# Score products of two heads on one array: 64-row matmuls and pairwise loads in a top-k attention kernel

## The chip, the cores and the metric

One core of a Trainium2 chip. The metric is device time in microseconds from the start of the program to its end. Engines are named as in the profile: PE is TensorE (PEld its weight loads), DVE is VectorE, ACT is ScalarE, POOL is GpSimd, SP issues the transfers.

## The reference

Attention in which each query keeps its 32 largest scores, followed by a gated feed-forward part over all rows. The first has batch 8, 8 heads, 576 rows and head size 64; the second 4608 rows, width 512 and inner width 1536.

```python
scores = scale * np.matmul(q, k.transpose(0, 1, 3, 2))
kth = np.partition(scores, -top_k, axis=-1)[..., -top_k:-top_k + 1]
scores = np.where(scores >= kth, scores, -1e9)
attn = softmax(scores)
x = np.matmul(attn, v)            # heads side by side: 4608 x 512
gate = 1.0 / (1.0 + np.exp(-(x @ w_gate)))
out = (gate * (x @ w_val)) @ w_out
```

All inputs and the output are float32.

## The kernel before, in words

**Tiles and steps.** A batch has four pairs of heads. For each pair the 576 rows are cut into four tiles of 128 and one of 64 (`i == NT`), in which both heads' last 64 rows share one tile. One pair and one tile make a step; there are 160, of them 128 with two full tiles (one per head) and 32 with last rows. `groups` gives their order: the first two batches are each cut into two groups (tiles 0 and 1, then 2 to 4), the other six batches are a group each. Within a group all tiles of a pair come before the next pair.

**Precision.** TensorE's fast format (float32r) holds fewer bits than float32, so a float32 operand is held as a high part (a rounded copy, made on ACT) and a low part (the rest, subtracted on POOL). Keys are loaded twice, one copy above the other on the 128 partitions; after the split (lines 147 and 148) the upper 64 partitions hold the high part and the lower 64 the low part. The queries of a step are loaded with the same doubling, 2 x 128 columns, and split into `qh` and `ql` over all partitions (lines 158 and 159). One matmul over 128 rows thus multiplies `qh` with both parts of the keys, a second one `ql`.

**Scores** (line 177). For each head, the 576 keys are cut into halves of 288, and each half takes two matmuls. A head's four matmuls fill the one score buffer in PSUM (`ps_s`, two banks), which ACT reads out with one copy (line 184) before the next head's may begin. The last-rows tile has ten matmuls in one go, as the second head's keys are rolled by 64 columns.

**Selection.** DVE finds the 32nd largest score of each row (lines 237 to 253, with a subtraction on POOL at line 249), ACT takes exponentials, and DVE masks and sums them (line 196). TensorE transposes the weights (line 273), and `weigh` multiplies them with the values (lines 289 to 298): one matmul whose 128 output rows serve both heads, the others with 64 output rows, one head in each half.

**Feed-forward part** (`ffn`, lines 331 to 361). A group's rows are ready when its last step is done. Its work is handed out in pieces between the steps, so that it stays 640 rows behind the attention (`BEHIND`). The weights, given in double precision, are split once near the start of the program and written to memory.

**Order of the work.** `fetch` asks for a pair's keys and values two steps ahead, `ask` for a step's queries four steps ahead, `begin` makes the scores two steps ahead (lines 369 to 400). All these loads are issued on SP, together with those of the feed-forward weights and the stores. From this order and a simulated timing, the compiler of the kernel's language fixes the order of each engine's instructions, which doesn't change at run time. Buffers are counted by the pools of lines 62 to 76.

If a row's count of scores lies outside its bounds, everything is computed a second time in a general way (lines 433 to 445).

Of the kernel before, what the change touches and what calls it, by code (L numbers as in the profile page):

```python
# [10 lines left out]
F32 = mybir.dt.float32  # L11
# [9 lines left out]
# scores are held times SHRINK, far under 1 (a power of two, exact)  # L21
SHRINK = 2.0**-60
# [4 lines left out]
def tile_topk_attention_then_gated_ffn(  # L27
# [10 lines left out]
    B, H, _, S = k.shape  # L38
    D = P // 2
    HALF = S // 2  # L40
    NP = H // 2
# [39 lines left out]
    # place of a row's 32nd largest among the 8 largest under the bound, by its count  # L81
# [58 lines left out]
    def load_keys(b, p, nm):  # L140
        """Both heads' transposed keys, a part over the other on the partitions, and their values."""
        ks = []
        for h in (2 * p, 2 * p + 1):
            raw = bkr.tile([P, S], F32, tag="kraw", name=f"kraw_{nm}_{h}")
            nc.sync.dma_start(raw, k[b, h])
            kt = bk.tile([P, S], F32R, tag="k", name=f"k_{nm}_{h}")
            nc.scalar.activation(kt, raw, AF.Copy)
            nc.gpsimd.tensor_tensor(kt[D:], raw[D:], kt[D:], op=ALU.subtract)
            ks.append(kt)
        vt = bv.tile([P, 11, D], F32, tag="v", name=f"v_{nm}")  # L150
        nc.sync.dma_start(vt, v[b, p].rearrange("p (c d) -> p c d", d=D))
        return ks, vt

    def load_queries(b, i, p):
        raw = bqr.tile([P, 2 * P], F32, tag="qraw", name=f"qraw_{b}_{i}_{p}")
        nc.sync.dma_start(raw, q[b, i, p])
        qh, ql = [bq.tile([P, 2 * P], F32R, tag=t, name=f"{t}_{b}_{i}_{p}") for t in ("qh", "ql")]
        nc.scalar.activation(qh, raw, AF.Copy)
        nc.gpsimd.tensor_tensor(ql, raw, qh, op=ALU.subtract)  # L159
        return qh, ql  # L160

    def scores(qs, ks, i, nm):
        """Scores of one tile of each head (i < NT), or of both heads' last rows in one tile."""
        J = 2 if i < NT else 1
        s = bs.tile([P, 2, S], F32, tag="s", name=f"s_{nm}")
        for j in range(J):
            ps = ps_s.tile([P, 2, 512], F32, tag="s", name=f"pss_{nm}_{j}")
            for half in range(2):
                # a head, the first column, their number, the first key
                parts = [(j, 0, HALF, half * HALF)]  # L170
                if i == NT:
                    # the second head's keys are rolled by REM
                    m = S - REM - HALF
                    parts += [(1, 0, HALF, REM)] if half == 0 else [(1, 0, m, REM + HALF), (1, m, REM, 0)]
# [189 lines left out]
    def run(general):  # L364
# [19 lines left out]
        for m in range(max(FETCH, ASK)):  # L384
            if m < FETCH:
                fetch(m)
# [109 lines left out]
```

## Time and profile before

| | |
|---|---|
| median of 3 runs | 1689.44 us |
| lowest and highest | 1687.72 and 1690.73 us |
| span of the profiled execution | 1685.6 us |
| the profiled execution's own time | listed as its span alone; 3.8 us under the median |
| mean granted TensorE clock | 0.976 of full speed |

The profile is of one execution; all its rows count microseconds from the first instruction. Busy time is a union: matmuls that overlap are counted once, so TensorE's cost of a matmul is read from the distance of its start to the next start. In a row such as `128*64 128x256` the first pair of numbers is the size of the weights (rows of the array by columns of output rows) and the second that of the moving operand.

### The profile page before, as it was taken

How to read it: one execution, taken by the hardware profiler on the slowest of the kernel's cores; microseconds unless marked ns; L12 is line 12 of the kernel's file. 1: busy time of each engine (PE TensorE's matmuls, PEld its weight loads, DVE VectorE, ACT ScalarE, POOL GpSimd, SP SyncE). 2: the span in 40 equal slices, each digit the busy share in tenths (PEclk: the TensorE clock that was granted, in tenths of full speed). 3: DMA queues.
4: the chain of work that ended last, by engine and by line, in shares of the span. 5: the costliest groups of instructions: out<-in, count | busy, mean ns of one | idle time of the engine just before them, and what ended most of it. 6: DMA issues, size and time to landing. Idle time of an engine off the chain costs nothing.

```text
span 1685.6 us, 36209 instructions
## 1 busy us (share of the span) xinstructions
PE 1575.0 (93%) x11506; PEld 1398.7 (83%) x11506; DVE 1521.8 (90%) x6802; ACT 1166.2 (69%) x2467; POOL 1052.7 (62%) x1187
## 2 busy tenths in 40 slices
PE   5665799999999989999999999999999999999998
PEld 2333598888989868998899999999999898999998
DVE  7999999999999999999999999999999999995000
ACT  7787777776777667776676767777776776765222
POOL 6766667767666766576764676576756675564233
PEclk8788899999999989999999999999999999999999
DMA  8777586756776543334433444434534353333543
GB/s 303 257 237 236 206 290 245 271 205 242 251 265 213 210 129 116 138 136 139 163 132 130 136 156 147 134 133 149 170 132 153 124 166 130 118 106 110 195 156 125
DMA packets 86026, 297.37 MB, mean 176 GB/s; under 512 B 9536, under 2 KB 38208, under 8 KB 62784
## 3 DMA queue, kind: packets, MB, share of 16 engines
q1 hardware_dynamic: 85824, 294.95, 51.1%
q8 instruction: 93, 1.52, 0.4%
q14 instruction: 109, 0.89, 0.2%
HBM read 266.60 MB, written 28.31 MB: 175 GB/s over the span
## 4 chain that ended last, share of the span: by engine, by line
PE 49%; DVE 35%; ACT 3%; issue 2%; POOL 1%; POOLq 0%; ACTq 0%; DVEq 0%
PE pz L332 8%; PE pz L331 8%; PE pz L333 8%; DVE e L196 7%; DVE cand L237 7%; DVE tops L252 5%; DVE over L248 5%; PE pss L177 5%; PE pt L273 4%; PE po L351 3%; PE po L353 3%; PE po L352 3%; DVE pick L253 3%; DVE tops L241 3%; PE po L292 3%; DVE cand L243 3%
## 5 line engine op out<-in xcount | busy, mean ns | idle before, releaser
L331 PE MATMUL pz<-xh,w 128*128 128x288 f32 (+2 forms) x1536 | 461.9, 301 | 3.1 <-DVE gf L337 1.5
L332 PE MATMUL pz<-xl,w 128*128 128x288 f32 (+2 forms) x1536 | 459.4, 299 | 0.1
L333 PE MATMUL pz<-xh,w 128*128 128x288 f32 (+2 forms) x1536 | 458.5, 299 | 0.0
L249 POOL TENSOR_TENSOR u<-s,over 128x1152 f32<-128x1152 f32 (+1 forms) x160 | 354.3, 2214 | 74.0 <-DVE over L248 70.2
L237 DVE MAX8 cand<-s 128x8 f32<-128x72 f32 x2304 | 355.3, 216 | 7.0 <-ACT s L184 6.7
L196 DVE SCALAR_TENSOR_TENSOR e<-s,st,e 128x576 f32<-128x576 f32 x288 | 300.8, 1065 | 0.1
L331 PEld LDWEIGHTS pz<-xh,w 128*128 128x128 f32 x1536 | 289.3, 188 | 9.0 <-issue 3.5
L332 PEld LDWEIGHTS pz<-xl,w 128*128 128x128 f32 x1536 | 289.2, 188 | 3.9 <-issue 3.5
L333 PEld LDWEIGHTS pz<-xh,w 128*128 128x128 f32 x1536 | 289.2, 188 | 2.7 <-issue 2.7
L202 ACT ACTIVATE e<-e,st 128x576 f32<-128x576 f32 x288 | 209.4, 771 | 83.1 <-DVE st L200 82.5
L339 POOL TENSOR_TENSOR gl<-gf,gh 128x288 fp32r<-128x288 f32 (+2 forms) x192 | 163.1, 850 | 153.7 <-ACT gh L338 145.8
L192 ACT ACTIVATE e<-s,st 128x576 f32<-128x576 f32 x288 | 210.2, 774 | 35.0 <-POOL st L190 34.1
L351 PE MATMUL po<-gh,w 128*128 128x288 f32 (+2 forms) x768 | 224.4, 302 | 6.3 <-DVE gf L337 3.9
L248 DVE TENSOR_SCALAR_CACHE_REDUCE over<-s,tops 128x576 bf16<-128x576 f32 x288 | 228.5, 798 | 1.1
L352 PE MATMUL po<-gl,w 128*128 128x288 f32 (+2 forms) x768 | 227.6, 299 | 0.6 <-POOL gl L339 0.5
L353 PE MATMUL po<-gh,w 128*128 128x288 f32 (+2 forms) x768 | 226.1, 297 | 0.0
L177 PE MATMUL pss<-k,qh 128*128 128x288 f32 (+2 forms) x672 | 199.7, 314 | 23.5 <-ACT s L184 16.4
L184 ACT ACTIVATE s<-pss 128x576 f32<-128x576 f32 x288 | 185.8, 645 | 47.2 <-PE pss L177 24.2
L252 DVE MAX8 tops<-u 128x8 f32<-128x576 f32 x288 | 204.3, 744 | 2.2 <-POOL u L249 1.4
L274 ACT ACTIVATE et<-pt 128x384 f32<-128x384 f32 x384 | 180.5, 491 | 35.5 <-PE pt L273 33.9
L273 PE MATMUL pt<-ident,e 128*128 128x128 f32 x1152 | 189.7, 281 | 7.7 <-ACT e L202 4.0
L177 PE MATMUL pss<-k,ql 128*128 128x288 f32 (+2 forms) x672 | 190.4, 302 | 0.4 <-POOL ql L159 0.4
(82 smaller groups left out, 3380.3 us busy)
## 6 DMA issues: line engine op xcount, KB each, us to landing
w<-ws SPq DMA_DIRECT2D x180, 1024.0 KB, 5.0
kraw<-in_k_dram SPq DMA_DIRECT2D x80, 288.0 KB, 3.2
qraw<-in_q_dram SPq DMA_DIRECT2D x160, 128.0 KB, 3.0
wraw<-in_w_dram SPq DMA_DIRECT2D x36, 512.0 KB, 5.0
ws<-wpair SPq DMA_DIRECT2D x36, 512.0 KB, 5.4
v<-in_v_dram SPq DMA_DIRECT2D x40, 352.0 KB, 3.8
out_dram<-acc SPq DMA_DIRECT2D x48, 144.0 KB, 2.3
out_dram<-acc SPq DMA_DIRECT2D x8, 160.0 KB, 4.1
```

Source lines behind the costliest of these rows:

```text
L177: nc.tensor.matmul(ps[:, half, o : o + n], x[:, h * P : (h + 1) * P], ks[h][:, k0 : k0 + n], start=t == 0, stop=t == len(todo) - 1,)
L196: nc.vector.scalar_tensor_tensor(e[:, j], s[:, j], kth[j], e[:, j], op0=ALU.is_ge, op1=ALU.mult, accum_out=st[:, 4 + j : 5 + j])
L237: nc.vector.max(cand[:, j, 8 * g : 8 * g + 8], s[:, j, g * SEG : (g + 1) * SEG])
L248: nc.vector.tensor_scalar(over[:, j], s[:, j], t, None, op0=ALU.is_ge, op1=ALU.add, accum_out=c)
L249: nc.gpsimd.tensor_tensor(u[:, :J], s[:, :J], over[:, :J], op=ALU.subtract)
L252: nc.vector.max(t, u[:, j])
L331: nc.tensor.matmul(ps, wt[:, u, 0, d], xh[:, cols], start=d == 0, stop=False)
L332: nc.tensor.matmul(ps, wt[:, u, 0, d], xl[:, cols], start=False, stop=False)
L333: nc.tensor.matmul(ps, wt[:, u, 1, d], xh[:, cols], start=False, stop=d == NP - 1)
L351: nc.tensor.matmul(ps, wt[:, e % 2, 0, f], gh, start=f == 0, stop=False)
L352: nc.tensor.matmul(ps, wt[:, e % 2, 0, f], gl, start=False, stop=False)
L353: nc.tensor.matmul(ps, wt[:, e % 2, 1, f], gh, start=False, stop=f == FG - 1)
```

## The change

Queries and keys of a pair of heads now lie one head above the other on the 128 partitions, without doubling. A pair's queries (640 columns: 512, and 64 for each head's last rows, with zeros in the other head's place), keys (576 columns) and values (15 blocks of 64 columns, 11 before) are loaded at once, four steps ahead, and split once into high and low parts over all partitions. A full tile's scores are made half by half of the keys: for each half, three products (high by high, high by low, low by high), and each of them as two matmuls of 64 rows, one per head, into two PSUM banks; ACT then reads out both heads' half. The product of the two low parts is left out. The last-rows tile takes three matmuls of 128 rows for each half of the keys, since the zeros keep the heads apart. The value products of the last rows use blocks 10 to 14.

```diff
-    FETCH, ASK, AHEAD = 2, 4, 2
+    FETCH, AHEAD = 4, 2
...
-    bk = ctx.enter_context(tc.tile_pool(name="bk", bufs=4))
-    bv = ctx.enter_context(tc.tile_pool(name="bv", bufs=3))
+    bk = ctx.enter_context(tc.tile_pool(name="bk", bufs=2))
+    bv = ctx.enter_context(tc.tile_pool(name="bv", bufs=2))
     bs = ctx.enter_context(tc.tile_pool(name="bs", bufs=4))
-    bq = ctx.enter_context(tc.tile_pool(name="bq", bufs=4))
-    bqr = ctx.enter_context(tc.tile_pool(name="bqr", bufs=3))
     bkr = ctx.enter_context(tc.tile_pool(name="bkr", bufs=2))
...
-    def load_keys(b, p, nm):
...
-    def load_queries(b, i, p):
...
+    def split(src, name, nm):
+
+        raw = bkr.tile([P, S + REM], F32, tag="raw", name=f"{name}raw_{nm}")[:, : src.shape[1]]
+        nc.sync.dma_start(raw, src)
+        high, low = [
+            bk.tile([P, src.shape[1]], F32R, tag=f"{name}{x}", name=f"{name}{x}_{nm}") for x in "hl"
+        ]
+        nc.scalar.activation(high, raw, AF.Copy)
+        nc.gpsimd.tensor_tensor(low, raw, high, op=ALU.subtract)
+        return high, low
+
+    def load(b, p, nm):
+
+        qs, ks = split(q[b, p], "q", nm), split(k[b, p], "k", nm)
+        vt = bv.tile([P, 15, D], F32, tag="v", name=f"v_{nm}")
         nc.sync.dma_start(vt, v[b, p].rearrange("p (c d) -> p c d", d=D))
...
     def scores(qs, ks, i, nm):
...
+        (qh, ql), (kh, kl) = qs, ks
+        products = [(qh, kh), (qh, kl), (ql, kh)]
         s = bs.tile([P, 2, S], F32, tag="s", name=f"s_{nm}")
...
+        rows = slice(i * P, (i + 1) * P)
+        if i < NT:
             for half in range(2):
...
+                cols = slice(half * HALF, (half + 1) * HALF)
+                ps = ps_s.tile([P, 2, 512], F32, tag="s", name=f"pss_{nm}_{half}")
+                for t, (x, y) in enumerate(products):
+                    for j in range(2):
+                        head = slice(j * D, (j + 1) * D)
+                        nc.tensor.matmul(
+                            ps[:, j, :HALF], x[head, rows], y[head, cols], start=t == 0, stop=t == 2
+                        )
+                nc.scalar.activation(s[:, :, cols], ps[:, :, :HALF], AF.Copy, scale=SCALE * SHRINK)
+        else:
+            ps = ps_s.tile([P, 2, 512], F32, tag="s", name=f"pss_{nm}")
+            for half in range(2):
+                cols = slice(half * HALF, (half + 1) * HALF)
+                for t, (x, y) in enumerate(products):
+                    nc.tensor.matmul(ps[:, half, :HALF], x[:, rows], y[:, cols], start=t == 0, stop=t == 2)
...
         def fetch(m):
             if m < len(steps) and steps[m][2] == groups[steps[m][0]][1]:
                 g, p, _ = steps[m]
-                keys[g, p] = load_keys(groups[g][0], p, f"{mark}{g}_{p}")
+                loaded[g, p] = load(groups[g][0], p, f"{mark}{g}_{p}")
...
             fetch(m + FETCH)
-            ask(m + ASK)
             begin(m + AHEAD)
```

## Rows read from the trace of the kernel before

**Rows 1.** Windows by stage: us, then each engine's busy us (count), PEclk, DMA share, GB/s

```profile
0.00:213.00 213.00, 136.13 (x537) 82.83 (x538) 202.59 (x710) 164.53 (x312) 138.03 (x134) 0.85 0.75 250
213.00:640.00 427.00, 406.67 (x3054) 363.51 (x3052) 426.33 (x1989) 312.00 (x667) 290.93 (x328) 0.98 0.65 227
640.00:1541.00 901.00, 893.78 (x6866) 816.40 (x6865) 879.22 (x4071) 648.94 (x1392) 581.53 (x672) 1.00 0.41 138
1541.00:1686.00 145.00, 138.38 (x1056) 135.95 (x1054) 13.62 (x35) 40.70 (x98) 42.17 (x54) 0.99 0.44 156
```

**Rows 2.** TensorE's timeline at 611 us: start, us, engine, line, operation, [idle before]

```profile
610.93 0.40 PE L177 MATMUL pss<-k,qh 128*128 128x288 f32 x1 [2.12 <-ACT s L184]
```

**Rows 3.** TensorE's timeline around 1006 us, across three changes of matmul shape

```profile
1005.69 0.29 PE L352 MATMUL po<-gl,w 128*128 128x288 f32 x1
1005.92 0.27 PE L295 MATMUL po<-et,v 128*64 128x64 f32 x1
1005.93 0.27 PE L296 MATMUL po<-et,v 128*64 128x64 f32 x1
1006.03 0.22 PE L295 MATMUL po<-et,v 128*64 128x64 f32 x1
...
1006.38 0.22 PE L295 MATMUL po<-et,v 128*64 128x64 f32 x1
...
1006.53 0.27 PE L297 MATMUL po<-et,v 64*64 64x64 f32 x1
...
1006.64 0.22 PE L297 MATMUL po<-et,v 64*64 64x64 f32 x1
...
1006.80 0.40 PE L177 MATMUL pss<-k,qh 128*128 128x288 f32 x1
1007.03 0.30 PE L177 MATMUL pss<-k,ql 128*128 128x288 f32 x1
```

**Rows 4.** TensorE's timeline around 605 us, a last-rows tile's score products

```profile
604.84 0.29 PE L177 MATMUL pss<-k,ql 128*128 128x288 f32 x1
604.97 0.27 PE L177 MATMUL pss<-k,qh 128*128 128x224 f32 x1
...
605.33 0.38 PE L331 MATMUL pz<-xh,w 128*128 128x288 f32 x1
```

**Rows 5.** Groups of instructions by form, GpSimd, 640 to 1541 us: two of line 249

```profile
L249 POOL TENSOR_TENSOR u<-s,over 128x1152 f32<-128x1152 f32 x78 | 190.6, 2444 | 43.1 <-DVE over L248 41.5 <-DVE st L200 0.8
...
L249 POOL TENSOR_TENSOR u<-s,over 128x576 f32<-128x576 f32 x20 | 26.9, 1343 | 6.2 <-DVE over L248 5.0 <-DVE st L200 1.0
```

**Rows 6.** Groups by form, TensorE, 213 to 640 us: two of line 177

```profile
L177 PE MATMUL pss<-k,qh 128*128 128x288 f32 x185 | 55.8, 317 | 8.5 <-ACT s L184 8.5
...
L177 PE MATMUL pss<-k,qh 128*128 128x224 f32 x11 | 3.0, 269 | 0.0
```

**Rows 7.** Timeline, all engines, around 904 us

```profile
903.63 0.22 DVE L253 SCALAR_TENSOR_TENSOR pick<-wanted,counts,tops 128x8 f32<-128x8 f32 x1
...
903.98 1.43 DVE L196 SCALAR_TENSOR_TENSOR e<-s,st,e 128x576 f32<-128x576 f32 x1
903.99 0.80 POOL L339 TENSOR_TENSOR gl<-gf,gh 128x288 fp32r<-128x288 f32 x1 [0.60 <-ACT gh L338]
...
905.33 0.81 DVE L196 SCALAR_TENSOR_TENSOR e<-s,st,e 128x576 f32<-128x576 f32 x1
```

**Rows 8.** Groups by form, whole span: count, busy us, mean ns

```profile
L196 DVE SCALAR_TENSOR_TENSOR e<-s,st,e 128x576 f32<-128x576 f32 x288 | 300.8, 1065 | 0.1
...
L253 DVE SCALAR_TENSOR_TENSOR pick<-wanted,counts,tops 128x8 f32<-128x8 f32 x288 | 128.5, 468 | 0.0
L159 POOL TENSOR_TENSOR ql<-qraw,qh 128x256 fp32r<-128x256 f32 x160 | 126.4, 791 | 28.5 <-ACT qh L158 23.5 <-issue 0.2
...
L148 POOL TENSOR_TENSOR k<-kraw,k 64x576 fp32r<-64x576 f32 x80 | 118.8, 1486 | 20.5 <-PE pss L177 3.9 <-DMA kraw<-in_k_dram 2.9 <-ACT k L147 2.6
```

**Rows 9.** DMA issues on SP: operation, count, KB each, median us to landing

```profile
v<-in_v_dram SPq DMA_DIRECT2D x40, 352.0 KB, 3.8
```

More of the change, by code (lines that the diff above doesn't have):

```diff
@@ L37, in tile_topk_attention_then_gated_ffn @@
     P = 128
-    B, H, _, S = k.shape
+    B, NP, _, S = k.shape
     D = P // 2
     HALF = S // 2
-    NP = H // 2
     NT = S // P
@@ L138, in split_weights @@
                     nc.sync.dma_start(w_split[idx][:, i], pair.bitcast(F32))
-    def load_keys(b, p, nm):
[L142 to L150, printed above, removed]
-        nc.sync.dma_start(vt, v[b, p].rearrange("p (c d) -> p c d", d=D))
-        return ks, vt
@@ L154, in load_queries @@
-    def load_queries(b, i, p):
[L155 to L160, printed above, removed]
+    def split(src, name, nm):
[7 more added lines that the diff above has]
+        return high, low
@@ L162, in scores @@
+    def load(b, p, nm):
+        qs, ks = split(q[b, p], "q", nm), split(k[b, p], "k", nm)
+        vt = bv.tile([P, 15, D], F32, tag="v", name=f"v_{nm}")
+        nc.sync.dma_start(vt, v[b, p].rearrange("p (c d) -> p c d", d=D))
+        return qs, ks, vt
     def scores(qs, ks, i, nm):
-        J = 2 if i < NT else 1
+        (qh, ql), (kh, kl) = qs, ks
+        products = [(qh, kh), (qh, kl), (ql, kh)]
         s = bs.tile([P, 2, S], F32, tag="s", name=f"s_{nm}")
-        for j in range(J):
-            ps = ps_s.tile([P, 2, 512], F32, tag="s", name=f"pss_{nm}_{j}")
+        rows = slice(i * P, (i + 1) * P)
+        if i < NT:
@@ L168, in scores @@
             for half in range(2):
[L170 to L174, printed above, removed]
-                todo = [(x, part) for part in parts for x in qs]
-                for t, (x, (h, o, n, k0)) in enumerate(todo):
-                    nc.tensor.matmul(
-                        ps[:, half, o : o + n],
-                        x[:, h * P : (h + 1) * P],
-                        ks[h][:, k0 : k0 + n],
-                        start=t == 0,
-                        stop=t == len(todo) - 1,
-                    )
+                cols = slice(half * HALF, (half + 1) * HALF)
@@ L184, in scores @@
             nc.scalar.activation(
[L185 removed]
+                s[:, 0].rearrange("p (a n) -> p a n", a=2), ps[:, :, :HALF], AF.Copy, scale=SCALE * SHRINK
             )
@@ L295, in weigh @@
                 nc.tensor.matmul(po[:D], vt[:, c], et[:, c, :REM], start=c == 0, stop=False)
-                nc.tensor.matmul(po[D:], vt[:, 6 + c], et[:, c, REM:P], start=c == 0, stop=False)
+                nc.tensor.matmul(po[D:], vt[:, 10 + c], et[:, c, REM:P], start=c == 0, stop=False)
             nc.tensor.matmul(po[:D], vt[:REM, 4], et[:REM, 4, :REM], start=False, stop=True)
-            nc.tensor.matmul(po[D:], vt[:REM, 10], et[:REM, 4, REM:P], start=False, stop=True)
+            nc.tensor.matmul(po[D:], vt[:REM, 14], et[:REM, 4, REM:P], start=False, stop=True)
         xf = b2.tile([P, 2 * P], F32, tag="xf", name=f"xf_{nm}")[:, :n]
@@ L365, in run @@
         steps = [(g, p, i) for g, (_, first, end) in enumerate(groups) for p in range(NP) for i in range(first, end)]
-        keys, qs, staged, xs = {}, {}, {}, [[] for _ in groups]
+        loaded, staged, xs = {}, {}, [[] for _ in groups]
         mark = "g" if general else ""
@@ L376, in begin @@
                 g, p, i = steps[m]
-                staged[m] = scores(qs.pop(m), keys[g, p][0], i, f"{mark}{groups[g][0]}_{i}_{p}")
-        def ask(m):
-            if m < len(steps):
-                g, p, i = steps[m]
-                qs[m] = load_queries(groups[g][0], i, p)
-        for m in range(max(FETCH, ASK)):
-            if m < FETCH:
-                fetch(m)
-            if m < ASK:
-                ask(m)
+                staged[m] = scores(*loaded[g, p][:2], i, f"{mark}{groups[g][0]}_{i}_{p}")
+        for m in range(FETCH):
+            fetch(m)
         for m in range(AHEAD):
@@ L413, in run @@
             if o != P:
-                weigh(et, keys[g, p][1], o, xs[g][p], (i - i % 2 - first) * P, nm)
+                weigh(et, loaded[g, p][2], o, xs[g][p], (i - i % 2 - first) * P, nm)
             at += (P if i < NT else REM) / NP
```

22 lines of the change are left out of this document (10 added, 12 removed).

## The prediction, made before the changed kernel was run

> **What bounds the kernel now.** I read the windows by stage first. They cut the span where the engines change places: at 213 us, when the feed-forward products begin, at 640 us, and at 1541 us, when VectorE's work ends [rows 1]. From 213 to 640 VectorE is busy 426.33 of 427 us and TensorE leaves 20 us free, so **VectorE sets this stage**. From 640 to 1541 TensorE is busy 893.78 of 901 us and VectorE leaves 22 us; from 1541 on TensorE is nearly alone. So **TensorE sets everything after 640 us**. The seam shows in TensorE's timeline: around 609 us it has no feed-forward work left and waits 2.12 us for a score tile [rows 2]. A busy share counts overlapping matmuls as one, so I take TensorE's cost from the starts in its timeline. There a 288-column score matmul takes 0.13 us until the next, from 604.84 to 604.97 us [rows 4].
>
> **Score products, before.** A full tile has 8 such matmuls, in two groups of 4 (one per head): 8 x 0.13 = 1.04 us a step. A last-rows tile has 10; its four short ones take 0.36 us, from 604.97 to 605.33 [rows 4]. After, a last-rows tile has 6 matmuls of 288 columns and all rows, so it loses these 0.36 us.
>
> **Score products, after.** A full tile has 12 matmuls of 64 rows, in two groups of 6 (one per half of the keys). If the two heads run at once, a group is 3 pairs, 3 x 0.13 = 0.39 us, against 0.52 us now: 0.26 us less a step. No row shows two row halves at once. The nearest are the value products, whose two column halves start 0.01 us apart; six pairs take the 0.35 us from 1006.03 to 1006.38, so 0.06 us each [rows 3]. I take the pairs as simultaneous.
>
> **Changing the array's shape** is what the diff doesn't show. Each such group now sits between matmuls of all 128 rows, since feed-forward work fills TensorE while the one score buffer is read out. What a change costs stands in [rows 3]. Going in, from 1005.69 to 1005.92 us, takes 0.23 instead of 0.13, and the first pair then takes 0.11 instead of 0.06: 0.15 us together. From 128 to 64 rows, 1006.38 to 1006.53 and on to 1006.64, much the same: 0.09 + 0.05. Coming out, 1006.64 to 1006.80 takes 0.16 instead of 0.06 and on to 1007.03 it takes 0.23 instead of 0.13: 0.20 us together. I read the second part as the new weights' load, no longer hidden behind the matmul ahead, and longer here since these weights are 128 columns wide, not 64. The new groups have 128 columns too, so I take 0.20 us for each way in (bounds 0.14 and 0.20) and for each way out: 0.40 us a group, 0.80 us a step. A full step is then 0.78 + 0.80 = 1.58 us, **0.54 us more than now**.
>
> The Trainium skill's page TensorEngine Tiling (Array Packing), Key Properties, says that a change of tiling mode, not of the tile alone, drains TensorE; that speaks against this change. By that rule the trace agrees: 0.09 to 0.10 us at each of the three changes, and the row adds the exposed weight load, which the page doesn't name. By the page's Theoretical Speedup alone (up to 2x for 64 rows), without the drain, the sum would be that of the first rival.
>
> **The sum after 640 us.** 78 full and 20 last-rows steps lie there [rows 5]: 78 x 0.54 = +42.1, 20 x 0.36 = -7.2. Other work can also cut into a group, at 0.40 us each time. Of 156 groups I take 12, between none and a quarter; the order is fixed at compile time and not known here: +4.8. Together **+40 us**, all on the engine that sets the end.
>
> **Before 640 us.** TensorE's own added work hides at first: from 213 to 640 it has about 38 full and 11 last-rows steps [rows 6]: twice 185 long matmuls less 11 x 6, by 8. That is 38 x 0.54 - 11 x 0.36 = +16.6 us against 20 us free. If that cover were gone, the 16.6 us would be paid. VectorE gains. A two-input VectorE operation that meets a GpSimd subtraction waits it out: one of line 196 took 1.43 us beside a 0.80 us subtraction, the next 0.81 [rows 7]. Over 288 operations with means of 1.065 and 0.468 us [rows 8], against 0.81 and 0.22 alone [rows 7], that is 73 + 71 = 144 us. The query and key subtractions are 126.4 + 118.8 = 245 us [rows 8] of GpSimd's 1053, its four windows summed [rows 1], so some 34 us of it. In a whole batch a pair's 2432 columns (5 x 256 and 2 x 576) become 1216, so half goes; 41% of GpSimd's time lies before 640: about -7. I take **-6 us**: bounds 0 (fewer, longer subtractions of some 1.5 us, by the 1.486 us of 576 columns, block longer) and -14 (all of the early share). After 640 the relief is worth nothing, since TensorE sets the pace.
>
> **Costed at nothing.** ScalarE copies half the columns, and it was busy 648.94 of 901 us; the score evictions keep their number and size. On SP's queue the query loads, one a step, become 40 of 320 KB, key loads halve to 40, and value loads, which now land in 3.8 us, grow from 352 to 480 KB [rows 9]; four steps of lead cover them (427 / 49 = 8.7 us each). With two value buffers instead of three, a value load of the short groups must wait for the value products of the pair two before. Behind it on SP stand the next query and key loads, weight loads and stores; the value tile's user is two pairs later, so I see no one late. If that cover goes, a wait of up to one step, 9 us, falls before 640. The two loads at the very start change the first scores by perhaps 1 us either way. The low-times-low product is gone from the sums; the second pass would only run if a row's count left its bounds.
>
> **Sum.** The profiled execution has a span of 1685.6 us; the median of the runs, 1689.4, is 3.8 above it, and I put the same 3.8 around the new span. 1689.4 + 40 - 6 = **1723 us**. Its own range: without cuts, with 0.14 us for the way in and the full relief, 78 x 0.42 - 7.2 - 14 = +12, 1701; with a quarter of the groups cut (39 x 0.40 = +15.6), pairs 0.01 us longer (78 x 6 x 0.01 = +4.7) and no relief, 42.1 - 7.2 + 15.6 + 4.7 = +55, 1745.
>
> **Rivals.**
> **A, no change of shape is paid (faster).** The score matmuls sit between others at full rate, and only the row count differs. Then 78 x -0.26 - 7.2 - 6 = -33.5: 1656. Against it: going from 128 to 64 rows at the same 64 columns did cost [rows 3]. The change gains as long as a way in and out together cost less than 0.21 us a group (78 x (2 x 0.21 - 0.26) = 13).
> **B, only the first 0.10 us of each change is paid.** The weights of the other row half are loaded while matmuls still run: 78 x (4 x 0.10 - 0.26) = +11, -7, +2 for cuts, -6: 1689, between 1680 and 1696. The rows show the load exposed at each change; that they show other shapes speaks for it. The Trainium skill's TensorE: Matmul & The Clock Gate, Part 3, has weight loads overlap running matmuls when the row group differs; by that rule this case would hold, and no run here shows it for rows.
> **C, the halves don't run at once, so the change doesn't do what it says.** One after another, 12 x 0.13 + 0.80 - 1.04 = +1.32 us a step: 78 x 1.32 - 7 + 5 = +101, and before 640 us 38 x 1.32 - 4 - 20 = +26, so about 1816. If only their weight loads take turns (2 x 0.10 us a pair, by the load exposed on the way out), 6 x 0.20 + 0.80 - 1.04 = +0.96 us a step gives 1689 + 72 + 13 = 1774. Against both: the column halves [rows 3].
>
> **Chances.** Forecast 0.60, A 0.13, B 0.15, C 0.12. The range goes from A, 1654, to the forecast's upper end, 1745; it leaves out C and some of the edges. A measurement here tells 0.2% (3.4 us) from no change. Faster: A and 0.05 of B, 0.18. Within: 0.06 of B. Slower: the forecast, C and 0.04 of B, 0.76.
>
> **What would show it.** In TensorE's timeline: two score matmuls starting within 0.01 us, pairs 0.13 us apart, and some 0.2 us lost ahead of and behind each group of six. TensorE still without idle time after the seam, the seam itself somewhat earlier than 640 us, VectorE's line 196 and 253 means lower. I am wrong if the groups enter and leave at 0.13 us, if the heads follow each other 0.13 us apart, or if TensorE has idle time after the seam.

## The result, and the profile after

The changed kernel took **1713.52 us** (median of 5 runs), the kernel before 1687.72 beside it: ratio **1.0146**, 95% interval 1.0131 to 1.0160, so some 25 us slower. 1723 us was forecast, in a range from 1654 to 1745. The first profile of the changed kernel fell in a disturbed run; the one read here is of a second measurement of the same kernel (1711.25 us, ratio 1.0129, interval 1.0112 to 1.0146).

> The changed kernel as it stands, profiled again at the higher granted clock. My theory (each group of 64-row matmuls costs 0.40 us for going in and out of its shape, on the engine that sets the pace after the seam): 1713 us, TensorE without idle time after the seam, the seam some 10 to 15 us earlier than 640 us, which makes up for the part of the forecast's +40 us that is not seen. Rival (fewer groups after the seam, or cheaper changes, than forecast): the seam stays at 640 us and the stage after it is only some 25 us longer.

Its windows by stage, cut at the same times as [rows 1], with the same columns:

```profile
0.00:213.00 213.00, 144.08 (x647) 81.41 (x648) 202.27 (x709) 156.76 (x291) 123.95 (x116) 0.86 0.75 253
213.00:640.00 427.00, 417.18 (x3155) 350.52 (x3154) 422.88 (x2004) 306.13 (x629) 260.43 (x283) 0.99 0.60 213
640.00:1541.00 901.00, 901.00 (x6878) 776.07 (x6877) 824.81 (x3963) 615.68 (x1265) 499.72 (x563) 1.00 0.36 126
1541.00:1709.00 168.00, 160.19 (x1217) 155.72 (x1216) 36.76 (x131) 53.77 (x125) 54.23 (x67) 0.99 0.42 147
```

From 640 to 1541 us TensorE is now busy in the whole 901 us, where it left 7 free before, and VectorE's spare time has grown from 22 to 76 us. TensorE also has more work left at 1541. The page's shares of the chain that ended last say the same, before and then after:

```profile
PE 49%; DVE 35%; ACT 3%; issue 2%; POOL 1%; POOLq 0%; ACTq 0%; DVEq 0%
```

```profile
PE 75%; DVE 17%; ACT 1%; issue 1%; POOL 0%; DMA 0%; POOLq 0%; DVEq 0%; ACTq 0%
```

**Cutting by work, not by time.** Windows at fixed times mix the two parts of the change, since the steps move. VectorE computes one reciprocal per step, and at the 60th both kernels have the same 5157 of 6912 feed-forward matmuls left (so do those of the experiments, three of them with 5155 or 5166). That makes it a mark at the same amount of work, close to the seam. Its row in VectorE's timeline, before and then after (start, us, engine, line, operation):

```profile
629.55 0.16 DVE L200 RECIPROCAL st<-st 128x1 f32<-128x1 f32 x1
```

```profile
622.25 0.15 DVE L198 RECIPROCAL st<-st 128x1 f32<-128x1 f32 x1
```

So up to the mark the change gains 7.3 us, less than the 10 to 15 that I had expected of the seam. From there to the end the kernel before takes 1685.6 - 629.55 = 1056.05 us and the changed one 1709.9 - 622.25 = 1087.65: a loss of 31.6. Together +24.3, the difference of the two spans. The windows on either side of the mark, for the kernel before:

```profile
0.00:630.00 630.00, 534.86 (x3539) 441.06 (x3539) 618.92 (x2642) 467.42 (x959) 421.88 (x455) 0.94 0.69 238
630.00:1685.60 1055.60, 1040.11 (x7967) 957.63 (x7967) 902.84 (x4161) 698.75 (x1509) 630.78 (x732) 1.00 0.41 140
```

And for the changed kernel:

```profile
0.00:622.00 622.00, 544.87 (x3691) 420.56 (x3691) 607.15 (x2627) 450.22 (x894) 374.40 (x390) 0.95 0.67 232
622.00:1709.90 1087.90, 1077.58 (x8201) 943.16 (x8201) 879.57 (x4178) 682.12 (x1414) 563.93 (x638) 1.00 0.37 128
```

Behind the mark TensorE's busy time grows by 37.5 us and its idle time falls from 15.5 to 10.3.

Ahead of the mark, the stretch from the end of the first step (its reciprocal at 45.6 us before, 47.2 after) is the one that VectorE sets. The kernel before:

```profile
46.00:629.60 583.60, 510.97 (x3472) 428.04 (x3472) 582.93 (x2506) 431.25 (x893) 391.22 (x416) 0.94 0.68 233
```

The changed kernel:

```profile
47.20:622.30 575.10, 520.57 (x3615) 409.17 (x3615) 570.98 (x2514) 417.55 (x837) 349.55 (x357) 0.96 0.65 228
```

VectorE is busy all but 0.7 us of it before and all but 4.1 after. Its busy time falls by 12 us and the stretch by 8.9 (629.55 - 45.6 = 583.95 and 622.25 - 47.2 = 575.05); the first step ends 1.6 us later.

**The change of shape, in TensorE's timeline of the changed kernel** (columns as in [rows 3]; `x2` stands for two matmuls of one form, here one per head). It answers to [rows 3] and [rows 4]:

```profile
991.78 0.49 PE L271 MATMUL pt<-ident,e 128*128 128x128 f32 x3
...
993.51 0.29 PE L172 MATMUL pss<-kh,ql 64*128 64x288 f32 x2
993.73 0.55 PE L271 MATMUL pt<-ident,e 128*128 128x128 f32 x3
...
997.17 0.40 PE L172 MATMUL pss<-kh,qh 64*128 64x288 f32 x2
997.41 0.29 PE L172 MATMUL pss<-kl,qh 64*128 64x288 f32 x1
997.63 0.70 PE L287 MATMUL po<-et,v 128*128 128x256 f32 x2
...
999.27 0.66 PE L276 MATMUL pt<-ident,e 128*128 128x128 f32 x4
999.85 0.39 PE L172 MATMUL pss<-kl,qh 64*128 64x288 f32 x1
999.86 0.52 PE L172 MATMUL pss<-kh,ql 64*128 64x288 f32 x2
...
1007.97 0.29 PE L351 MATMUL po<-gh,w 128*128 128x288 f32 x1
1008.10 0.29 PE L349 MATMUL po<-gh,w 128*128 128x288 f32 x1
1008.32 0.40 PE L172 MATMUL pss<-kh,qh 64*128 64x288 f32 x2
1008.56 0.29 PE L172 MATMUL pss<-kl,qh 64*128 64x288 f32 x2
1008.69 0.29 PE L172 MATMUL pss<-kh,ql 64*128 64x288 f32 x2
1008.92 0.40 PE L350 MATMUL po<-gl,w 128*128 128x288 f32 x1
1009.15 0.29 PE L351 MATMUL po<-gh,w 128*128 128x288 f32 x1
```

Read the starts, as in the prediction. From 1007.97 to 1008.10 two full matmuls lie 0.13 us apart. Going into the group takes 0.22 and the first pair 0.24; the second pair takes 0.13; going out takes 0.23 and the first matmul behind it 0.23. That is 0.40 us over four times 0.13, for one group. This group is no exception: behind the mark the median is 0.22 us over 134 ways in from a feed-forward product and over 124 ways out into one. The two heads do run at once: at 999.85 and 999.86 a matmul of each head starts 0.01 us after the other. The weight loads (PEld) show what the second delay is:

```profile
1007.97 0.19 PEld L349 LDWEIGHTS po<-gh,w 128*128 128x128 f32 x1
1008.32 0.18 PEld L172 LDWEIGHTS pss<-kh,qh 64*128 64x128 f32 x2 [0.16 <-ACT et L272]
...
1008.91 0.19 PEld L350 LDWEIGHTS po<-gl,w 128*128 128x128 f32 x1 [0.16 <-issue]
1009.02 0.19 PEld L351 LDWEIGHTS po<-gh,w 128*128 128x128 f32 x1
```

The matmul at 1008.10 has its load at 1007.97 and the one at 1009.15 at 1009.02, so 0.13 us ahead. The first load behind each change starts with its own matmul, at 1008.32 and 1008.91, so it isn't made ahead of it.

Before a transposition the way out is cheaper: 0.22 us, and then three transpositions that take 0.55 instead of 0.49, so 0.15. The rows from 997.17 to 999.86 are a **cut group**: value products and transpositions were put between its third and fourth matmul, and the shape is changed four times instead of twice.

Counted along TensorE's timeline behind the mark, the shape changes 558 times, 204 times before. Three shapes are told apart here: products over all rows, transpositions among them; the 64-row score products; and the value products with 64 output rows, all as one. The 156 groups are entered 197 times, so 41 times one was cut.

VectorE's two lines that answer to [rows 8] (count, busy us, mean ns):

```profile
L194 DVE SCALAR_TENSOR_TENSOR e<-s,st,e 128x576 f32<-128x576 f32 x288 | 273.0, 969 | 0.5
...
L251 DVE SCALAR_TENSOR_TENSOR pick<-wanted,counts,tops 128x8 f32<-128x8 f32 x288 | 122.1, 445 | 0.2
```

And GpSimd's subtractions by form:

```profile
L145 POOL TENSOR_TENSOR ql<-qraw,qh 128x640 fp32r<-128x640 f32 x40 | 65.5, 1638 | 31.3 <-ACT qh L144 28.3 <-DVE cand L241 2.0
L145 POOL TENSOR_TENSOR kl<-kraw,kh 128x576 fp32r<-128x576 f32 x40 | 61.7, 1541 | 0.5
```

The subtractions went from 245 to 127 us, and VectorE's two lines from 429.3 to 395.1, so by 34.

### The profile page after: what moved, and what is told of

The parts are those of the page before. It is cut to its first block, busy times and chain, and to the rows that moved or that the text cites. A ratio compares the mean times of both kernels' runs of the same rounds, so it can differ in the third digit from the quotient of the medians.

```text
span 1798.6 us, 36066 instructions
## 1 busy us (share of the span) xinstructions
PE 1724.1 (96%) x11890; PEld 1437.0 (80%) x11890; DVE 1496.3 (83%) x6802; ACT 1140.4 (63%) x2307; POOL 936.5 (52%) x1027
## 4 chain that ended last, share of the span: by engine, by line
PE 85%; DVE 7%; ACT 1%; issue 1%; POOL 0%; DMA 0%; POOLq 0%; DVEq 0%; ACTq 0%
PE pz L329 12%; PE pz L330 12%; PE pz L331 12%; PE pss L172 8%; PE pt L271 8%; PE po L349 6%; PE po L350 6%; PE po L351 6%; PE po L290 5%; PE po L289 4%; PE po L287 2%; PE pss L181 1%; DVE cand L235 1%; DVE e L194 1%; PE pt L276 1%; PE po L293 1%
## 5 line engine op out<-in xcount | busy, mean ns | idle before, releaser
L329 PE MATMUL pz<-xh,w 128*128 128x288 f32 (+2 forms) x1536 | 483.4, 315 | 0.0
L330 PE MATMUL pz<-xl,w 128*128 128x288 f32 (+2 forms) x1536 | 481.2, 313 | 0.5 <-POOL xl L301 0.5
L331 PE MATMUL pz<-xh,w 128*128 128x288 f32 (+2 forms) x1536 | 479.2, 312 | 0.0
L329 PEld LDWEIGHTS pz<-xh,w 128*128 128x128 f32 x1536 | 295.1, 192 | 14.3 <-issue 11.6
L331 PEld LDWEIGHTS pz<-xh,w 128*128 128x128 f32 x1536 | 297.0, 193 | 5.7 <-issue 5.0
L194 DVE SCALAR_TENSOR_TENSOR e<-s,st,e 128x576 f32<-128x576 f32 x288 | 275.5, 978 | 0.5
L350 PE MATMUL po<-gl,w 128*128 128x288 f32 (+2 forms) x768 | 237.9, 312 | 0.0
L349 PE MATMUL po<-gh,w 128*128 128x288 f32 (+2 forms) x768 | 236.1, 317 | 0.4 <-ACT part L356 0.4
L351 PE MATMUL po<-gh,w 128*128 128x288 f32 (+2 forms) x768 | 236.4, 310 | 0.0
L335 DVE SCALAR_TENSOR_TENSOR gf<-gf,pz 128x288 f32<-128x288 f32 (+2 forms) x192 | 85.6, 446 | 176.2 <-PE pz L331 172.8
L175 ACT ACTIVATE s<-pss 128x576 f32<-128x576 f32 x256 | 165.8, 648 | 78.2 <-PE pss L172 66.3
L271 PE MATMUL pt<-ident,e 128*128 128x128 f32 x1152 | 204.7, 296 | 2.1 <-ACT e L200 1.7
L271 PEld LDWEIGHTS pt<-ident,e 128*128 128x128 f32 x1152 | 143.9, 145 | 31.8 <-issue 17.4
```

The lines of the kernel that those rows point to most:

```text
L194: nc.vector.scalar_tensor_tensor(e[:, j], s[:, j], kth[j], e[:, j], op0=ALU.is_ge, op1=ALU.mult, accum_out=st[:, 4 + j : 5 + j])
L271: nc.tensor.transpose(pt[:, c], ef[:, k0 : k0 + P], ident)
L329: nc.tensor.matmul(ps, wt[:, u, 0, d], xh[:, cols], start=d == 0, stop=False)
L330: nc.tensor.matmul(ps, wt[:, u, 0, d], xl[:, cols], start=False, stop=False)
L331: nc.tensor.matmul(ps, wt[:, u, 1, d], xh[:, cols], start=False, stop=d == NP - 1)
L349: nc.tensor.matmul(ps, wt[:, e % 2, 0, f], gh, start=f == 0, stop=False)
```

## The experiments

The theory: behind the mark TensorE pays about 0.2 us for each change of shape, and this alone turns a gain into the loss; ahead of it GpSimd's shorter work relieves VectorE a little. The rivals: the loss comes from elsewhere (the order, the buffers, the loads), or the gain ahead of the mark does. All ratios are to the kernel before, timed beside it, with 95% intervals. Windows have the columns of [rows 1] and are cut at each kernel's own 60th reciprocal.

**Three matmuls over all 128 rows, without a change of shape.** Both heads' rows are multiplied in one, so the heads are mixed.

```diff
-                    for j in range(2):
-                        head = slice(j * D, (j + 1) * D)
-                        nc.tensor.matmul(
-                            ps[:, j, :HALF], x[head, rows], y[head, cols], start=t == 0, stop=t == 2
-                        )
+                    j = t // 2
+                    nc.tensor.matmul(
+                        ps[:, j, :HALF], x[:, rows], y[:, cols], start=t != 1, stop=t != 0
+                    )
```

> A full tile's 6 matmuls of 64 rows per half become 3 of all 128 rows, so nothing of the pairs' length changes but the shape no longer does; the scores then mix the two heads. My theory: the whole price of the shape goes, 78 x 0.80 + 5 for cuts = 67 us after the seam: about 1646 us. Rival (the loss comes from the new loads, buffers or order): it stays within 10 us of 1713.

Measured: 1643.25 us, ratio 0.9724 (0.9708 to 0.9740).

```profile
0.00:618.00 618.00, 522.81 (x3389) 425.62 (x3389) 603.64 (x2630) 449.41 (x893) 379.19 (x389) 0.92 0.67 233
618.00:1640.90 1022.90, 1009.07 (x7733) 929.05 (x7733) 870.47 (x4173) 672.62 (x1415) 563.08 (x638) 0.99 0.39 136
```

The pairs of the changed kernel lie 0.13 us apart, as these single matmuls do, so what differs on TensorE is the shape. It changes 202 times behind the mark instead of 558, and TensorE's busy time there is 1077.58 - 1009.07 = 68.5 us shorter: **0.19 us a change**. Counted by the size of the weights alone (586 changes against 238) it is 0.20. Without the changes the kernel gains what rival A stood for, and 13 us more than its 1656: 11 us of its gain lie ahead of the mark, where A had 6, and 34 behind it, where A had 27.5.

**Six matmuls over all rows.** As many matmuls as in the changed kernel, but one after the other and without a change of shape. The heads are mixed here too.

```diff
-                        head = slice(j * D, (j + 1) * D)
...
-                            ps[:, j, :HALF], x[head, rows], y[head, cols], start=t == 0, stop=t == 2
+                            ps[:, j, :HALF], x[:, rows], y[:, cols], start=t == 0, stop=t == 2
```

> A full tile's 6 matmuls of 64 rows per half stay 6, each over all 128 rows: no shape change and no two at once; the scores then mix the two heads. 12 x 0.13 = 1.56 us a step against 1.58 us with pairs and changes of shape. My theory: 1713 us within 8 us, the pairs' gain is just eaten up by the changes. Rival (a change costs only its first 0.10 us): pairs then cost 1.18 us a step, and this kernel is 78 x 0.38 = 30 us slower than the changed one, about 1743.

Measured: 1709.23 us, ratio 1.0117 (1.0101 to 1.0134).

```profile
0.00:626.00 626.00, 550.93 (x3702) 460.51 (x3702) 612.63 (x2642) 451.46 (x896) 373.44 (x390) 0.95 0.66 230
626.00:1706.80 1080.80, 1067.50 (x8189) 990.10 (x8189) 871.31 (x4162) 677.66 (x1412) 562.22 (x637) 1.00 0.37 128
```

Behind the mark TensorE is busy 58.4 us longer than with three matmuls; three more of 0.13 us in 156 groups make 60.8. So a group's changes of shape (0.40 us and a share of the cuts) cost at least what the three pairs save (0.39): behind the mark TensorE is busy 10 us longer in the changed kernel (1077.58 us), which its earlier mark (3.7 us) and less idle time (10.3 against 13.3 us) nearly make up for. Running two heads at once is worth nothing here, because every group pays for its way in and out.

**Groups kept whole.** The six matmuls of a group are given priority at compile time, so that less is put between them.

```diff
-                for t, (x, y) in enumerate(products):
+                with tc.high_priority():
+                    for t, (x, y) in enumerate(products):
...
```

> The changed kernel with the score matmuls of a full tile given priority in the compile-time order, so that other work seldom cuts into a group of six: the groups are entered 158 times after the seam instead of 200, and 254 times instead of 312 in all. My theory: 42 entries fewer after the seam at some 0.36 us each (0.20 in, 0.15 to 0.20 out) take 15 us off: 1696 us, still slower than before the change. Rival (cuts are free because the work that cuts in is itself of another shape or fills a wait): within 4 us of 1711.

Measured: 1699.92 us, ratio 1.0069 (1.0052 to 1.0086), so 11 us less than the changed kernel. The shape changes 484 times behind the mark, 74 fewer; at 0.19 us that is 14 us. Behind the mark lie 912 of the groups' matmuls, so 152 groups, and they are entered 152 times: none is cut. The mark comes 5.5 us later than in the changed kernel, and the time from there to the end is 18.6 us shorter.

The control for this is the same priority on the score matmuls of the kernel **before**, whose groups have no shape of their own:

```diff
-                for t, (x, (h, o, n, k0)) in enumerate(todo):
+                with tc.high_priority():
+                    for t, (x, (h, o, n, k0)) in enumerate(todo):
...
```

> The kernel before the change with the same priority for the score matmuls as in the kernel that keeps its groups whole; no group changes the array's shape here. My theory: the priority is worth nothing by itself, within 4 us of 1689, so that the gain of 11 us in the changed kernel is that of the entries saved. Rival (the order itself is better with priority): some 11 us off, 1678.

Measured: 1714.15 us, ratio 1.0148 (1.0131 to 1.0165). A miss: I had expected nothing.

```profile
0.00:641.00 641.00, 553.75 (x3576) 452.80 (x3576) 628.76 (x2665) 470.80 (x972) 427.89 (x459) 0.92 0.68 234
641.00:1711.00 1070.00, 1041.63 (x7932) 958.85 (x7930) 907.54 (x4138) 689.53 (x1496) 636.37 (x729) 0.99 0.40 138
```

TensorE's busy time behind the mark is the same (1041.63 and 1040.11) and so nearly are its changes of shape (200 and 204; 253 and 234 by the size of the weights alone); what grows is its idle time, from 15.5 to 28.4 us, and the mark comes 11 us later. The 11 us ahead of it are VectorE's: between the first step and the mark it is busy 593.3 us instead of 582.9. Another order can thus cost 25 us with the same work. The 11 us that the whole groups gain are net of whatever the order costs there, and their number is no clean price of a cut.

**Both halves of a step in one run.** Four score banks instead of two, so that a full step goes in and out once. The four banks come from the other pools: one bank for the transpositions (two before) and two for the feed-forward products (three before).

```diff
-    ps_s = ctx.enter_context(tc.tile_pool(name="ps_s", bufs=1, space=bass.MemoryType.PSUM))
-    ps_t = ctx.enter_context(tc.tile_pool(name="ps_t", bufs=2, space=bass.MemoryType.PSUM))
+    ps_s = ctx.enter_context(tc.tile_pool(name="ps_s", bufs=2, space=bass.MemoryType.PSUM))
+    ps_t = ctx.enter_context(tc.tile_pool(name="ps_t", bufs=1, space=bass.MemoryType.PSUM))
...
-    ps_f = ctx.enter_context(tc.tile_pool(name="ps_f", bufs=3, space=bass.MemoryType.PSUM))
+    ps_f = ctx.enter_context(tc.tile_pool(name="ps_f", bufs=2, space=bass.MemoryType.PSUM))
...
-            for half in range(2):
+            pss = [ps_s.tile([P, 2, 512], F32, tag="s", name=f"pss_{nm}_{half}") for half in range(2)]
+            for half, ps in enumerate(pss):
+                cols = slice(half * HALF, (half + 1) * HALF)
+                with tc.high_priority():
...
+            for half, ps in enumerate(pss):
```

> Both halves' groups of a full tile are issued in one run into four PSUM banks instead of two (the transposes have one buffer instead of two, the feed-forward products two instead of three), with priority in the order as well: 105 entries after the seam instead of 200. My theory: 95 x 0.36 = 34 us off the changed kernel, 1677 us, faster than before the change, unless the fewer banks cost what they do in the kernel with fewer banks alone. Rival (the fewer banks stall TensorE after the seam): slower than 1711, with idle time on TensorE.

Measured: 1803.42 us, ratio 1.0680 (1.0662 to 1.0698), where I had expected 1677 unless the banks cost something.

```profile
0.00:649.00 649.00, 552.69 (x3693) 427.17 (x3694) 622.53 (x2678) 452.50 (x892) 379.60 (x390) 0.93 0.64 222
649.00:1801.50 1152.50, 1083.36 (x8198) 947.48 (x8198) 935.76 (x4125) 672.91 (x1416) 581.01 (x637) 0.98 0.35 120
```

The changes of shape fell to 435, but what gave the banks is short of them. The control takes the same banks from the changed kernel (the edits of `ps_t` and `ps_f` alone) and gives nothing for them:

> The changed kernel with one buffer for the transposes instead of two and two for the feed-forward products instead of three, and nothing else: the price of the banks by itself. My theory: a few us, 1711 to 1722, since TensorE always finds other work. Rival: tens of us, with idle time on TensorE.

Measured: 1826.86 us, ratio 1.0822 (1.0804 to 1.0840).

```profile
0.00:668.00 668.00, 568.24 (x3702) 428.45 (x3702) 629.64 (x2665) 458.81 (x900) 381.96 (x391) 0.93 0.62 216
668.00:1823.30 1155.30, 1099.05 (x8189) 951.50 (x8189) 941.19 (x4138) 679.91 (x1408) 557.02 (x636) 0.98 0.35 120
```

A miss, as I had expected a few us: the two banks alone cost 115 us. The mark comes 46 us later, and behind it TensorE stands idle for 56.3 us instead of 10.3 and is busy 21.5 us longer. Against this control the single run is 23 us faster. 136 fewer changes of shape (435 against 571) would give 26 us at 0.19, but the windows don't bear that out: 19 us of the gain lie ahead of the mark and 3 behind it, where those changes were counted. There TensorE is busy 15.7 us less and idle 12.9 us more. Priority is in it as well, so this pair doesn't price a way in and out. A third division of the banks left the feed-forward products their three and let the transpositions and the value products share one, the rest being as in the single run:

```diff
-    ps_o = ctx.enter_context(tc.tile_pool(name="ps_o", bufs=1, space=bass.MemoryType.PSUM))
+    ps_o = ps_t
...
-        po = ps_o.tile([P, 2 * P], F32, tag="o", name=f"po_{nm}")[:, :n]
+        po = ps_o.tile([P, 4 * P], F32, tag="t", name=f"po_{nm}")[:, :n]
```

> Both halves' groups in one run into four score banks, with priority, as in the kernel with one whole run, but the feed-forward products keep their three buffers, and the transposes and the value products share a single one. 100 entries after the seam instead of 200. My theory (it was the feed-forward products' third buffer that cost over 100 us): 100 x 0.30 = 30 us off 1711, 1681, if the shared buffer costs under 10 us. Rival (the transposes' buffer is what costs): above 1750, with TensorE's idle time ahead of the transposes.

Measured: 1957.2 us, ratio 1.1582 (1.1562 to 1.1601), where I had expected 1681. Its waits of TensorE and of VectorE name the place (us in total, times, longest):

```profile
PE pt L274 <- ACT et L275: 87.0, 111, 2.6
...
DVE e L197 <- ACT e L193: 85.9, 40, 6.8
```

The first row is a transposition that waits until ScalarE has read out an earlier one: 111 times, 87 us in all (3.5 us in the kernel before). Neither of these two divisions of the banks leaves room for a longer run.

**GpSimd's part.** To price the subtractions of queries and keys, each was made twice (into a spare buffer first):

```diff
+        spare = bkr.tile([P, S + REM], F32, tag="spare", name=f"{name}spare_{nm}")[:, : src.shape[1]]
+        nc.gpsimd.tensor_tensor(spare, raw, high, op=ALU.subtract)
         nc.gpsimd.tensor_tensor(low, raw, high, op=ALU.subtract)
```

> The changed kernel with each of the two low-part subtractions of a load made twice, the first into a spare tile, so that GpSimd subtracts as many columns as before the change. My theory: VectorE, which sets the stage before the seam, loses what the change gave it there, 6 to 15 us; the stage after it doesn't change: 1720 to 1728 us. Rival (the relief is worth nothing, since fewer but longer subtractions block as much): within 3 us of 1713.

Measured: 1763.29 us, ratio 1.0443 (1.0426 to 1.0460), so 52 us over the changed kernel, far outside what either theory gave.

```profile
66.00:662.20 596.20, 525.13 (x3596) 412.87 (x3595) 585.51 (x2487) 408.56 (x818) 399.79 (x387) 0.93 0.61 214
```

That is the stretch from the first step to the mark. By parts, against the changed kernel: the first step ends 19 us later (66.4 instead of 47.2 us), with four pairs' doubled subtractions ahead of it instead of three pairs' single ones (GpSimd is busy 49.6 us up to there instead of 24.9, VectorE 55.5 instead of 36.5); this stretch is 21 us longer, 14.5 of it VectorE's busy time; behind the mark it is 8 us. The order was also computed anew, so this is no clean price of the work. Taking the subtractions away is the other direction; the low parts become scaled copies on ScalarE:

```diff
-        nc.gpsimd.tensor_tensor(low, raw, high, op=ALU.subtract)
+        nc.scalar.activation(low, raw, AF.Copy, scale=2.0**-12)
```

> The changed kernel with the low parts written by ScalarE as scaled copies instead of subtracted on GpSimd, so that GpSimd has no query or key subtractions left (the low products are then wrong). My theory: VectorE sets the stage before the seam and loses its remaining waits for these subtractions there, 5 to 10 us off: 1701 to 1706. Rival (the stage before the seam is set by TensorE now): within 3 us of 1711.

Measured: 1695.76 us, ratio 1.0039 (1.0025 to 1.0053), 15 us under the changed kernel, more than the 5 to 10 that I had expected. The same stretch:

```profile
33.00:609.00 576.00, 522.81 (x3644) 410.70 (x3645) 555.06 (x2552) 444.86 (x887) 291.23 (x322) 0.96 0.66 234
```

And the same edit in the kernel before:

```diff
-            nc.gpsimd.tensor_tensor(kt[D:], raw[D:], kt[D:], op=ALU.subtract)
+            nc.scalar.activation(kt[D:], raw[D:], AF.Copy, scale=2.0**-12)
...
-        nc.gpsimd.tensor_tensor(ql, raw, qh, op=ALU.subtract)
+        nc.scalar.activation(ql, raw, AF.Copy, scale=2.0**-12)
```

> The kernel before the change with the low parts of queries and keys written by ScalarE as scaled copies instead of subtracted on GpSimd (the low products are then wrong): its 245 us of subtractions go, where the changed kernel without its 125 us gained 15.5 us. My theory (the relief before the seam goes with the GpSimd time taken away): 25 to 32 us off 1689, 1657 to 1664, all before the seam. Rival (fewer but longer subtractions block as much, so halving them gave the change nothing): about 15 us off, 1674, as in the changed kernel.

Measured: 1670.80 us, ratio 0.9879 (0.9859 to 0.9900).

```profile
34.00:617.00 583.00, 517.26 (x3496) 426.92 (x3496) 559.78 (x2543) 487.08 (x1011) 297.15 (x322) 0.94 0.70 239
```

It lies between what the theory gave (1657 to 1664) and the rival's 1674. This was the surprise: VectorE loses 23 us of busy time against the kernel before (582.93 to 559.78) and 16 against the changed one, and yet the stretch is as long as it was: 583.0 against 583.6 us, 576.0 against 575.1. VectorE now has 21 to 23 us of idle time in it; ScalarE, which took the copies over, is busy for 56 us more in the kernel before and 27 in the changed one. Most of what both gain (11.7 of 15.1 us and 14.0 of 16.0, by the spans) they gain ahead of the first step, which ends at 33.9 instead of 45.6 us and at 33.2 instead of 47.2. So with the subtractions gone VectorE no longer sets this stretch alone. In the kernel before, its waits there are for ScalarE (10.6 us), GpSimd (7.5) and TensorE (2.6). Part of that is the edit's own doing, as ScalarE has more to do; what the stretch would take with the relief and no such work isn't shown.

**The two ways side by side.** If the gain lies ahead of the mark and the loss behind it, the new way for batches 0 to 2 (60 steps) and the old one for batches 3 to 7 should beat both kernels.

This kernel has the changed kernel's two value buffers, and its old way asks for queries three steps ahead, not four.

```diff
...
+                if b < CUT:
+                    staged[m] = scores(*loaded[g, p][:2], i, f"{mark}{b}_{i}_{p}")
+                else:
+                    staged[m] = scores2(qs.pop(m), loaded[g, p][1], i, f"{mark}{b}_{i}_{p}")
...
```

> The changed kernel's way (loads a pair at a time, 64-row score products) for batches 0 to 2, and the way of the kernel before (step-wise query loads, doubled keys, products over all rows) for batches 3 to 7; both layouts of queries and keys are given as inputs, and the results are the same as in either kernel up to the product of the low parts. The first three batches are 60 steps, so the switch lies at about the point where VectorE stops to set the pace. Theory (the gain comes before the seam, where TensorE's extra work hides; the loss after it, from changes of shape): 8 us gained before, nothing lost behind: 1681 us, in the ratio 0.995, below both kernels; VectorE's 60th reciprocal at 622 to 626 us, and some 200 changes of shape after it, not 558. Rival one (the first part gains only as part of the whole order, or the third batch's loads in the old way, which fall before the seam, give it back): 1689 us within 3, reciprocal at 630. Rival two (the switch costs buffers or waits of its own): over 1695 us, with idle time of TensorE after the seam.

Measured: 1684.15 us, ratio 0.9969 (0.9958 to 0.9981). It does beat both, by 5 us of the 8 expected.

```profile
44.10:630.20 586.10, 524.63 (x3616) 415.44 (x3617) 582.41 (x2536) 419.97 (x844) 351.31 (x360) 0.94 0.64 226
...
630.00:1682.20 1052.20, 1039.10 (x7965) 959.36 (x7963) 900.52 (x4168) 695.15 (x1507) 635.32 (x732) 0.99 0.41 143
```

But the gain isn't where the theory put it. The mark comes at 630.2 us, as before, so rival one is right about the first part: GpSimd has as little to do in it as in the changed kernel (351.31 and 349.55 us), and VectorE is as busy as in the kernel before (582.41 and 582.93). The gain lies behind the mark, 4 us (1052.0 against 1056.05): 1 us less of TensorE's busy time and some 2.5 less of its idle time, with 200 changes of shape, 4 fewer than before. The loss behind the mark is avoided, as the theory has it; why these last 4 us came (the order, the buffers, the query loads) isn't settled.

## Why the prediction was right in the main, and where it was off

The sum was +40 behind the seam and -6 ahead of it; the traces show +31.6 and -7.3, cut at the mark.

- **The price of a change of shape** (0.20 us each way, 0.40 a group) is what the timeline shows in the new groups, and the kernel without them gives 0.19 a change. All changes together were put at 62.4 + 4.8 = 67.2 us; that kernel says 68.5.
- **The cuts** were mis-sized: 12 groups were taken, and 41 were cut, 0.40 us x 29 = 11.6 more, just over the upper bound of a quarter. Two things that the prediction didn't count make up for it. 52 of the ways out lead to a transposition, which costs 0.05 us less (-2.6). And 40 of the 394 ways in and out replace a change that was there anyway, as they lie next to value products: 394 - 354 more changes in all, 40 x 0.20 = -8. Then 67.2 + 11.6 - 2.6 - 8 = 68.2. That this term came out was partly luck.
- **The products themselves** were put at 78 x -0.26 - 7.2 = -27.5; the kernel with three full matmuls has 1040.11 - 1009.07 = -31.0 us of TensorE's busy time behind the mark. With the shape that makes +37.5, against the +39.7 of the sum.
- **The step that failed** is "all on the engine that sets the end". TensorE had 15.5 us of idle time behind the mark, 7 of them between 640 and 1541 us [rows 1], and I let none of it take up new work. 5.2 us went that way (15.5 to 10.3; none is left from 640 to 1541). So +37.5 became +32 in time: this and the busy time explain the 8 us that +40 was too high. The sign that I had named, no idle time after the seam, holds up to 1541 us; 1.6 of the 10.3 us lie before 640 and the rest behind 1541, where the kernel before has 6.3 of its own.
- **VectorE's relief** (-6, bounds 0 and -14) has the right size, -8.9 in the stretch and +1.6 at the start, but this is luck: its reason, GpSimd's time in proportion, fell. Between the first step and the mark GpSimd works about 40 us less in the changed kernel, in both kernels with full rows and in the one with both ways (349.55, 352, 348 and 351.31, against 391.22), and VectorE's busy time falls by 12, 16, 7 and 0.5 us; the mark comes anywhere from 618.5 to 630.2 us. How much the two engines meet seems to be a matter of the order, which isn't shown by a run of its own and can't be read from the trace of before; only the bounds could be had. The size of the whole effect was probably underrated too: in the kernel before without the subtractions, whose order is another, lines 196 and 253 take 254.4 + 95.9 = 350.3 us instead of 429.3, 79 less, where I had put 34.
- **After 640 us the relief is worth nothing**: nearly so. Without the subtractions the time behind the mark is 2.8 us shorter in the kernel before (1053.3 against 1056.05) and 2.5 in the changed one (1085.15 against 1087.65).
- **TensorE's added work ahead of the seam is hidden**: from 213 to 640 us its busy time grew by 10.5 us and 9.8 us of idle time are left; VectorE remains busy there for 422.88 of 427 us. That agrees, though a kernel with the same loads and no cover gone wasn't tried.
- **Costed at nothing**: the loads. The waits of the changed kernel's trace name one for these loads, 1.2 us of ScalarE's for a query load. On the page, the values land 0.3 us later than before (3.8), the queries 0.8 (3.0) and the keys, though of the same size, 1.3 (3.2 before); the four steps of lead cover it:

```profile
v<-in_v_dram SPq DMA_DIRECT2D x40, 480.0 KB, 4.1
...
qraw<-in_q_dram SPq DMA_DIRECT2D x40, 320.0 KB, 3.8
```

**The rivals.** A (no change of shape paid) and B (only the first 0.10 us) fell by the timeline: 0.22 and then 0.24 us on the way in, 0.23 and 0.23 on the way out; the six full matmuls took 1709 us, where the expectation had 1743 for a change of 0.10 us. The Trainium skill's TensorE: Matmul & The Clock Gate, Part 3, by which weight loads overlap running matmuls of another row group, agrees inside a group (the second pair follows after 0.13 us, as matmuls over all rows do) and doesn't describe the change of shape, where the load isn't made ahead. The Trainium skill's page TensorEngine Tiling (Array Packing), Key Properties, has a change of mode drain TensorE; the rows agree again, with 0.09 to 0.10 us for the first of the two delays, for which the page gives no time. C (the halves one after the other) fell by the starts at 999.85 and 999.86 us.

**Open:** what a cut costs in time (keeping the groups whole gained 11 us, but priority itself cost 25 in the control); what made the mark come earlier or later; which orders let VectorE and GpSimd meet less; and a step's two halves in one run with banks to spare, which this kernel's PSUM doesn't leave.

## What to carry to other kernels

A product on part of the array's rows paid on every way in and out here, 0.40 us a group, the price of three 288-column matmuls: count the groups, and what will stand around them, before counting the columns saved. Compare two traces at a mark of equal work, not at equal times, and take out of the forecast the idle time that the bounding engine still has. Where the compiler orders the work anew, that alone can move the time (25 us in one control here), so run a control that has the new order without the new work.

## What the runs showed of the hardware

- A change between full rows and half the rows, or back, takes 0.09 to 0.10 us in which no new matmul starts, and the next matmul's successor comes 0.10 to 0.11 us late; before a transposition this second part is 0.06 us. Over the 356 changes that the kernel with three full matmuls lacks: 0.19 us each.
- Two matmuls on the two halves of the rows, into two PSUM banks, start 0.01 us apart, and such pairs of 288 columns follow each other in the 0.13 us of one matmul.
- Two PSUM banks fewer (one of two for transpositions, one of three for the feed-forward products) cost 115 us; going from six 64-row matmuls a group to three full ones, the largest gain here, is worth 68.
- A VectorE operation of line 196, 0.81 us by itself, took up to 2.94 us beside a 2.84-us GpSimd subtraction of line 249; line 194 of the changed kernel up to 3.01. Still, when the query and key subtractions went to ScalarE as copies and VectorE, which had been busy for 99.9% of a stretch, lost 23 us of busy time there, the stretch took as long as before (ScalarE was busy 56 us more).
- Priority for the score matmuls of the kernel before, with the same work and nearly the same changes of shape, cost 25 us.
